# Joining weight bits with two one-input 16-bit passes, and normalising both attention heads on GpSimd

## The chip, the cores and the metric

The kernel runs on one core of a Trainium2 chip. The metric is the device time of one execution in microseconds; lower is better. The core has TensorE (PE, with PEld for its weight loads), VectorE (DVE), ScalarE (ACT), GpSimd (POOL) and the queues that issue transfers (here SyncE, SP). Each engine works through its own instructions in program order and waits for others on semaphores.

## The reference, cut to what matters

```python
def attention(q, k, v):                     # batch 2, 12 heads, 448 positions, head size 64
    scores = causal_mask(q @ k.T / 8)       # masked entries: -1e9
    scores = scores - scores.max(-1)
    attn = exp(scores)
    attn = attn / (attn.sum(-1) + 1e-9)     # the normalising
    return attn @ v                         # 896 tokens x 768

def moe(x):                                 # w_in 768x2048, w_out 2048x768
    h = x @ w_in
    return (h * clip(h + 3, 0, 6) / 6) @ w_out

def moe2(x):                                # w_gate, w_val 768x1536, w_out 1536x768
    xn = x / sqrt(mean(x*x) + 1e-6) * rms_g
    return (silu(xn @ w_gate) * (xn @ w_val)) @ w_out

out = moe2(moe(attention(q, k, v)))
```

The weights arrive as 64-bit floats, q, k and v as 32-bit floats.

## The kernel before, in words

**Attention.** The work is cut into 24 units, each one batch, one pair of heads (j = 0 and 1) and one half g of the 448 query positions. Units 0 to 11 have g = 0 and rows of 112 and 224 keys (blocks i = 0 and 1), units 12 to 23 have g = 1 and rows of 336 and 448 keys. A unit goes through `a_scores` (S below: TensorE, L232), `a_mask` (DVE, L242, adds the mask and takes the row's extreme), `a_exp` (ACT, L249, which also sums the row), `a_sums` (DVE, L257 and L258: the reciprocals of the sums), `a_norm` (L268: each row times its reciprocal; head 0 on DVE, head 1 on GpSimd, two instructions a head), `a_transpose` (T below: TensorE, L284, one call a head), `a_evict` (ACT, L294, copies the transposed rows out of PSUM), `a_values` (V below: TensorE, L310), `a_x` (ACT, L320) and `a_xlow` (DVE, L326).

**Weights.** Each piece of the weights is a tile `raw` of 128 x 768 64-bit floats, seen as 768 pairs of 32-bit words, low and high. `w_split` makes a 32-bit float of each: ACT scales the high words into `c` (L134), DVE shifts the low words right by 29 (L135) and joins the sign bit of the high words to them (L136, two inputs), and a step later `w_join` shifts `c` left by 3 and joins these bits (L141). ACT then rounds `c` into `whi` (L150), and DVE takes `wlo` = c - whi (L156). 68 pieces are made in this way; 32 more are pieces kept in DRAM that come back as 32-bit floats and go straight to L150.

**Products.** Each product of the two networks is three matmuls (L174, L176, L178) on the high and low parts. Networks run after one another for the two halves g; the first product for g = 0 starts when the units with g = 0 are through, beside the attention of g = 1.

**Order.** The program order is written out by hand in steps. `at(delay, fn)` puts a call into a later step; within a step come first the calls that are due, then what `plan` holds for the step. Unit u starts at step 5u, with S there. T and V come at fixed steps after it, and `a_sums` at a fixed number of steps after `a_exp`, by a table over five phases (phase 0: units 0 to 8; phases 4, 3, 2: units 9, 10, 11; phase 1: units 12 to 20):

```python
SUMS = (4, 1, 1, 2, 3)
TRANSPOSES = (12, 8, 6, 9, 11)
VALUES = (19, 13, 9, 13, 17)
...
        at(0, a_norm, u, 0)
        at(1, a_norm, u, 1)
```

So T(0) stands on TensorE's queue between S(2) and S(3), and in general T(u) ahead of S(u+3) for the early units. From unit 9 on the distance between the normalising and T is shorter. No product stands on TensorE's queue before S(13); from there on 4.8 matmuls of the products are issued in each step beside the attention.

Of the kernel before, what the change touches and what calls it, by code (L numbers as in the profile page):

```python
# [9 lines left out]
F32 = mybir.dt.float32  # L10
F32R = mybir.dt.float32r
U32 = mybir.dt.uint32
AF = mybir.ActivationFunctionType
ALU = mybir.AluOpType

# [27 lines left out]
def fused_kernel(ctx: ExitStack, tc, qa, qb, ka, kb, v, w_in, w_out, w_gate, w_val, w_out2, rms_g, out):  # L43
# [5 lines left out]
    nc = tc.nc  # L49
# [10 lines left out]
    def slot(shape, name, dtype=F32):  # L60
        return pool.tile(shape, dtype, tag="a", name=name)

    def f32(ap):
        return ap.bitcast(F32)
# [15 lines left out]
    def at(delay, fn, *args):  # L80
        due[clock["now"] + delay].append((fn, args))
# [24 lines left out]
    def w_load():  # L106
# [4 lines left out]
        if srcs[n] is None:  # L111
# [3 lines left out]
            return  # L115
        t = wpool.tile([128, 768, 2], U32, tag="raw", name=f"raw{n}", bufs=NRAW)
        nc.sync.dma_start(t.rearrange("p n t -> p (n t)"), srcs[n].bitcast(U32))
        raws[n] = t

    def w_split():  # L120

        n = state["split"]
        if n >= len(srcs):
            return
        state["split"] += 1
        if n in plain:
            at(1, w_halves, n, plain.pop(n))
            return
        raw = raws.pop(n)
        low, high = raw[:, :, 0], raw[:, :, 1]  # L130
        c = wpool.tile([128, 768], F32, tag="c", name=f"c{n}", bufs=NC_BUF)


        nc.scalar.mul(c, f32(high), 2.0 ** -112)  # L134
        nc.vector.tensor_scalar(low, low, 29, None, op0=ALU.logical_shift_right)  # L135
        nc.vector.scalar_tensor_tensor(low, high, 0x80000000, low, ALU.bitwise_and, ALU.bitwise_or)  # L136
        at(1, w_join, n, c, low)

    def w_join(n, c, z):
        bits = c.bitcast(U32)  # L140
        nc.vector.scalar_tensor_tensor(bits, bits, 3, z, ALU.logical_shift_left, ALU.bitwise_or)  # L141
        if n < 4 * NP1:
            kept[n + NP1] = dram.tile([128, 768], F32, name=f"kept{n}")
            nc.sync.dma_start(kept[n + NP1], c)
        at(1, w_halves, n, c)
# [16 lines left out]
    def w_tile(n, j):  # L162

        if n not in used:
            used.add(n)
            splits.pop(n - 2, None)
            at(1, w_split)
        return tuple(t[:, j * 128:(j + 1) * 128] for t in splits[n])
# [78 lines left out]
    def a_exp(u, outs, last):  # L247
        for c, src, dst, n in outs:
            nc.scalar.activation(  # L249
                dst, dst, AF.Exp, scale=-1.0, bias=st[u][:, 0, c:c + 1],  # L250
                accum_out=st[u][:, 1, c:c + 1])
# [3 lines left out]
    def a_sums(u):  # L255
        t = st[u]
        nc.vector.tensor_scalar_add(t[:, 2], t[:, 1], 1e-9)  # L257
        nc.vector.reciprocal(t[:, 2], t[:, 2])  # L258
        at(0, a_norm, u, 0)
        at(1, a_norm, u, 1)  # L260

    def a_norm(u, j):
        g, b, p = units[u]
        for i in range(2):
            n = (2 * g + i + 1) * C
            t, o = sm[u, j][i]
            c = st[u][:, 2, 2 * j + i:2 * j + i + 1]
            (nc.vector, nc.gpsimd)[j].tensor_scalar_mul(t[:, o:o + n], t[:, o:o + n], c)  # L268

    def a_transpose(u, j):  # L270
        g, b, p = units[u]
# [69 lines left out]
    def ff1_relu(g, m, ps):  # L341
        t = slot([128, NT], f"t{g}_{m}")
        nc.scalar.activation(t, ps, AF.Relu, bias=half, scale=1.0 / 6.0)
        at(1, ff1_mul, g, m, ps, t)
# [27 lines left out]
    def ff1_y(g, m, ps):  # L372
        hi = slot([128, NT], f"yhi{g}_{m}", F32R)
        nc.scalar.mul(hi, ps, gvec[:, m:m + 1])
        s = slot([128, NT], f"sq{g}_{m}")
        nc.scalar.activation(s, ps, AF.Square)
        at(1, ff1_ylow, g, m, ps, hi, s)
# [17 lines left out]
    def rms_root(g, ps):  # L395
        nc.scalar.activation(ri[g], ps, AF.Sqrt, bias=eps, scale=1.0 / DM)
        at(1, rms_inv, g)
# [26 lines left out]
    def ff2_silu(t):  # L424
        nc.scalar.activation(t, t, AF.Silu)

# [36 lines left out]
    with tc.manual_schedule():  # L463
# [41 lines left out]
        for n in range(NW - 1):  # L505
            plan[30 + 16 * n].append((0, w_split))
# [73 lines left out]
```

## Time and profile before

| | us |
|---|---|
| median of 3 runs | 614.26 (614.22 to 614.49) |
| profiled execution, whole time | 613.24 |
| profiled execution, span from first to last instruction | 611.5 |
| mean granted TensorE clock | 0.992 |
| TensorE busy | 599.3 (98%) |
| DVE busy | 430.4 (70%) |
| ACT busy | 303.4 (50%) |
| POOL busy | 122.3 (20%) |

The shares are means over stages that differ: attention alone (to about 53 us), attention beside the first product (to about 166 us), and products alone (to the end).

### The profile page before, as it was taken

To read this page: it belongs to the slowest core of one execution; us is meant where nothing else is said; L and a number is where in the kernel's file an instruction comes from. 1 tells how busy PE (TensorE), PEld (TensorE's weight loads), DVE (VectorE), ACT (ScalarE), POOL (GpSimd) and SP (SyncE) were. 2 spreads that over 40 slices of the span, in tenths; PEclk is the share of its full clock that TensorE was granted. 3 is DMA by queue.
4 is the path that set the end of the run, shared out by engine and by line. 5 is a ranking of instruction groups with operands and counts; after the bars stand their busy time and mean duration, and the time that the engine had idled before them with its cause. 6 is when DMAs were issued, how large, how long until landed. Compare 5 with 4: busy or idle time off the path is not lost.

```text
span 611.5 us, 8863 instructions
## 1 busy us (share of the span) xinstructions
PE 599.3 (98%) x3210; PEld 521.1 (85%) x3210; DVE 430.4 (70%) x763; ACT 303.4 (50%) x599; POOL 122.3 (20%) x108
## 2 busy tenths in 40 slices
PE   8879999999999999999999999999999999999997
PEld 6545767676899999999999999999999999999996
DVE  4879999998444499995444977777777777555520
ACT  5978878787644565554333653343334344222200
POOL 3434333241123331011010111111111112100000
PEclk9889999999999999999999999999999999999999
DMA  8468758564133648985435523332333333244100
GB/s 226 135 205 239 252 182 275 179 219 133 59 98 108 229 154 284 330 295 179 126 86 206 194 96 117 103 105 103 104 104 107 114 116 124 96 144 144 53 32 30
DMA packets 31931, 92.98 MB, mean 152 GB/s; under 512 B 4624, under 2 KB 13648, under 8 KB 31888
## 3 DMA queue, kind: packets, MB, share of 16 engines
q1 hardware_dynamic: 31888, 92.42, 46.3%
q8 instruction: 25, 0.41, 0.3%
q14 instruction: 18, 0.15, 0.1%
HBM read 77.07 MB, written 15.34 MB: 151 GB/s over the span
## 4 chain that ended last, share of the span: by engine, by line
PE 93%; ACT 4%; DVE 1%; DMA 0%; issue 0%; POOL 0%; DVEq 0%; ACTq 0%; POOLq 0%
PE f L174 10%; PE f L178 9%; PE f L176 9%; PE h L176 7%; PE h L178 7%; PE h L174 6%; PE y L174 6%; PE y L178 6%; PE y L176 6%; PE o L174 5%; PE o L178 5%; PE o L176 5%; PE s L232 4%; PE o L310 4%; PE t L284 3%; ACT sm L249 3%
## 5 line engine op out<-in xcount | busy, mean ns | idle before, releaser
L150 ACT CAST whi<-c 128x768 fp32r<-128x768 f32 x100 | 83.5, 835 | 125.7 <-DVE c L141 106.8
L156 DVE TENSOR_TENSOR wlo<-c,whi 128x768 fp32r<-128x768 f32 x100 | 97.1, 971 | 23.6 <-ACT whi L150 21.6
L174 PE MATMUL f<-yhi,whi 128*128 128x448 f32 x288 | 105.8, 367 | 0.0
L178 PE MATMUL f<-yhi,wlo 128*128 128x448 f32 x288 | 104.9, 364 | 0.0
L176 PE MATMUL f<-ylo,whi 128*128 128x448 f32 x288 | 104.0, 361 | 0.0
L268 POOL TENSOR_SCALAR sm<-sm,st 112x112 f32<-112x112 f32 (+3 forms) x48 | 54.9, 1154 | 100.3 <-DVE st L258 29.1
L136 DVE SCALAR_TENSOR_TENSOR raw<-raw 128x768 uint32<-128x768 uint32 x68 | 73.1, 1075 | 2.3
L176 PE MATMUL h<-xl,whi 128*128 128x448 f32 x192 | 72.1, 375 | 0.0
L174 PE MATMUL h<-xh,whi 128*128 128x448 f32 x192 | 71.3, 371 | 0.0
L178 PE MATMUL h<-xh,wlo 128*128 128x448 f32 x192 | 71.0, 370 | 0.0
L174 PE MATMUL y<-ghi,whi 128*128 128x448 f32 x192 | 70.5, 367 | 0.0
L178 PE MATMUL y<-ghi,wlo 128*128 128x448 f32 x192 | 70.0, 365 | 0.0
L176 PE MATMUL y<-glo,whi 128*128 128x448 f32 x192 | 69.3, 361 | 0.0
L141 DVE SCALAR_TENSOR_TENSOR c<-c,raw 128x768 uint32<-128x768 uint32 x68 | 65.8, 968 | 2.7 <-ACT c L134 0.4
L134 ACT ACTIVATE c<-raw 128x768 f32<-128x768 f32 x68 | 61.9, 910 | 1.3 <-DMA raw<-in_w_out 1.3
L358 POOL TENSOR_TENSOR slo<-u,shi 128x448 fp32r<-128x448 f32 x24 | 31.2, 1300 | 145.8 <-ACT shi L436 145.8
L178 PEld LDWEIGHTS f<-yhi,wlo 128*128 128x128 f32 x288 | 53.9, 187 | 5.4 <-issue 0.2
L176 PEld LDWEIGHTS f<-ylo,whi 128*128 128x128 f32 x288 | 54.1, 188 | 4.0
L174 PEld LDWEIGHTS f<-yhi,whi 128*128 128x128 f32 x288 | 54.1, 188 | 3.7 <-issue 0.2
L249 ACT ACTIVATE sm<-sm,st 112x112 f32<-112x112 f32 (+3 forms) x96 | 49.7, 519 | 14.6 <-DVE st L242 14.5
L174 PE MATMUL o<-shi,whi 128*128 128x448 f32 x144 | 52.9, 367 | 0.0
L178 PE MATMUL o<-shi,wlo 128*128 128x448 f32 x144 | 52.3, 363 | 0.0
(61 smaller groups left out, 929.3 us busy)
## 6 DMA issues: line engine op xcount, KB each, us to landing
raw<-in_w_out SPq DMA_DIRECT2D x28, 768.0 KB, 5.0
raw<-in_w_in SPq DMA_DIRECT2D x16, 768.0 KB, 5.1
kept<-c SPq DMA_DIRECT2D x32, 384.0 KB, 2.7
c<-kept SPq DMA_DIRECT2D x32, 384.0 KB, 3.1
raw<-in_w_gate SPq DMA_DIRECT2D x12, 768.0 KB, 4.4
raw<-in_w_val SPq DMA_DIRECT2D x12, 768.0 KB, 4.3
k<-in_kb SPq DMA_DIRECT2D x24, 112.0 KB, 4.3
v<-in_v SPq DMA_DIRECT2D x12, 224.0 KB, 3.8
```

The source lines that it names most:

```text
L134: nc.scalar.mul(c, f32(high), 2.0 ** -112)
L136: nc.vector.scalar_tensor_tensor(low, high, 0x80000000, low, ALU.bitwise_and, ALU.bitwise_or)
L141: nc.vector.scalar_tensor_tensor(bits, bits, 3, z, ALU.logical_shift_left, ALU.bitwise_or)
L150: nc.scalar.copy(hi, c)
L156: nc.vector.tensor_sub(lo, c, f32(hi))
L174: nc.tensor.matmul(ps, whi, xhi, start=first, stop=False)
L176: nc.tensor.matmul(ps, whi, xlo, start=False, stop=False)
L178: nc.tensor.matmul(ps, wlo, xhi, start=False, stop=last)
L232: nc.tensor.matmul(ps[:C, o:o + n], tq[64 * j:64 * j + 64, i * C:(i + 1) * C], tk[64 * j:64 * j + 64, 0:n], start=True, stop=True)
L249: nc.scalar.activation(dst, dst, AF.Exp, scale=-1.0, bias=st[u][:, 0, c:c + 1], accum_out=st[u][:, 1, c:c + 1])
L268: (nc.vector, nc.gpsimd)[j].tensor_scalar_mul(t[:, o:o + n], t[:, o:o + n], c)
L358: (engine or nc.gpsimd).tensor_sub(lo, t, f32(hi))
```

## The change

The two DVE passes that prepare the low words become two passes over 16-bit words with one input each. Word 1 of the four 16-bit words of a 64-bit float, shifted right by 13, goes to word 0; the top bit of word 3 goes to word 1. The 32-bit low word then holds the same bits as before. And `a_norm` runs on GpSimd for both heads, as one instruction with two multiplications: by the row's reciprocal, then by 1.0.

```diff
+U16 = mybir.dt.uint16
...
         nc.scalar.mul(c, f32(high), 2.0 ** -112)
-        nc.vector.tensor_scalar(low, low, 29, None, op0=ALU.logical_shift_right)
-        nc.vector.scalar_tensor_tensor(low, high, 0x80000000, low, ALU.bitwise_and, ALU.bitwise_or)
+
+        words = raw.rearrange("p n t -> p (n t)").bitcast(U16).rearrange("p (n w) -> p n w", w=4)
+        nc.vector.tensor_scalar(words[:, :, 0], words[:, :, 1], 13, None, op0=ALU.logical_shift_right)
+        nc.vector.tensor_scalar(words[:, :, 1], words[:, :, 3], 0x8000, None, op0=ALU.bitwise_and)
         at(1, w_join, n, c, low)
...
-            (nc.vector, nc.gpsimd)[j].tensor_scalar_mul(t[:, o:o + n], t[:, o:o + n], c)
+            nc.gpsimd.tensor_scalar(t[:, o:o + n], t[:, o:o + n], c, 1.0, op0=ALU.mult, op1=ALU.mult)
```

## Rows read from the trace of the kernel before

**Rows 1.** The page: busy times by engine, and the chain that ended last.
```profile
PE 599.3 (98%) x3210; PEld 521.1 (85%) x3210; DVE 430.4 (70%) x763; ACT 303.4 (50%) x599; POOL 122.3 (20%) x108
...
PE 93%; ACT 4%; DVE 1%; DMA 0%; issue 0%; POOL 0%; DVEq 0%; ACTq 0%; POOLq 0%
```

**Rows 2.** Busy time by stretch: engines in us, granted clock, DMA share, GB/s.
```profile
0.00:50.00 50.00, 42.30 (x304) 29.16 (x304) 35.99 (x171) 38.25 (x141) 19.05 (x34) 0.90 0.68 198
50.00:100.00 50.00, 49.12 (x299) 34.85 (x299) 49.30 (x112) 40.60 (x96) 19.70 (x12) 1.00 0.71 228
```

**Rows 3.** The same columns, by single microseconds.
```profile
25.00:26.00 1.00, 1.00 (x6) 0.81 (x6) 1.00 (x3) 1.00 (x6) 0.00 (x0) 0.59 0.92 257
...
32.00:33.00 1.00, 1.00 (x13) 0.58 (x10) 0.26 (x2) 1.00 (x4) 0.54 (x1) 0.99 0.94 346
```

**Rows 4.** Timeline of TensorE: start, duration, instructions, idle time before and releaser.
```profile
24.89 1.35 PE L284 MATMUL t<-ident,sm 112*112 112x112 f32 x6 [1.76 <-DVE sm L268]
...
38.42 1.69 PE L310 MATMUL o<-pt,v 112*64 112x224 f32 x8 [2.54 <-ACT pt L294]
...
50.88 0.78 PE L310 MATMUL o<-pt,v 112*64 112x224 f32 x6 [1.10 <-ACT pt L294]
```

**Rows 5.** Lines 135 and 136: duration in ns, min/median/max.
```profile
L135 DVE TENSOR_SCALAR raw<-raw x68: 532/555/1532, 20.6 to 579.3; 128x768 uint32<-128x768 uint32 x68
...
L136 DVE SCALAR_TENSOR_TENSOR raw<-raw x68: 958/961/1801, 21.2 to 579.9; 128x768 uint32<-128x768 uint32 x68
```

**Rows 6.** The chain that ended last, 34 to 37 us: start, us, what.
```profile
34.20 0.43 DVE sm L268 x2
34.64 0.48 DVE raw L135
...
35.14 0.97 DVE raw L136
...
36.21 0.97 DVE c L141
```

**Rows 7.** Timeline of DVE: a normalising that stands ahead of the next mask.
```profile
42.43 0.62 DVE L268 TENSOR_SCALAR sm<-sm,st 112x112 f32<-112x112 f32 x2
```

**Rows 8.** Groups of POOL by form, 5 to 22 us: busy us, mean ns.
```profile
L268 POOL TENSOR_SCALAR sm<-sm,st 112x224 f32<-112x224 f32 x5 | 4.2, 844 | 0.0
L268 POOL TENSOR_SCALAR sm<-sm,st 112x112 f32<-112x112 f32 x5 | 2.8, 566 | 11.2 <-DVE st L242 10.0 <-DVE st L258 1.2
```

**Rows 9.** Groups of POOL by form, 74 to 160 us.
```profile
L268 POOL TENSOR_SCALAR sm<-sm,st 112x448 f32<-112x448 f32 x9 | 14.7, 1634 | 0.0
L268 POOL TENSOR_SCALAR sm<-sm,st 112x336 f32<-112x336 f32 x9 | 12.3, 1364 | 58.7 <-ACT pt L294 16.5 <-PE o L310 14.8 <-DVE st L258 9.3
```

**Rows 10.** POOL over the whole span: two memsets, by form.
```profile
L474 POOL MEMSET mask<- 112x448 f32 x1 | 0.5, 472 | 0.0
...
masks.py:197 POOL MEMSET ident<- 128x128 f32 x1 | 0.2, 205 | 0.3 <-POOLq L569 0.3
```

**Rows 11.** Line 386: an addition of two tensors on POOL, ns min/median/max.
```profile
L386 POOL TENSOR_TENSOR sq<-sq,sq x10: 1153/1165/1442, 250.4 to 346.3; 128x448 f32<-128x448 f32 x10
```

**Rows 12.** Timeline of the first units, 9 to 14 us.
```profile
9.11 1.39 POOL L268 TENSOR_SCALAR sm<-sm,st 112x112 f32<-112x112 f32 x2 [6.97 <-DVE st L242]
...
9.83 0.80 DVE L268 TENSOR_SCALAR sm<-sm,st 112x112 f32<-112x112 f32 x2
...
11.24 0.24 DVE L242 CUSTOM_DVE_ANT_0 sm<-s,mask 112x112 f32<-112x112 f32 x1
...
11.30 0.83 PE L232 MATMUL s<-k,q 64*112 64x112 f32 x8
...
13.64 0.24 DVE L242 CUSTOM_DVE_ANT_0 sm<-s,mask 112x112 f32<-112x112 f32 x1
```

**Rows 13.** Timeline of unit 12: head 1's normalising on POOL, head 1's T.
```profile
51.95 2.97 POOL L268 TENSOR_SCALAR sm<-sm,st 112x336 f32<-112x336 f32 x2 [4.86 <-DVE st L258]
...
55.75 0.45 PE L284 MATMUL t<-ident,sm 112*112 112x112 f32 x3
```

## The prediction

> **What bounds the kernel now.** I read the page first. TensorE is busy for 98% of the span and makes up 93% of the chain that ended last [rows 1], so a faster DVE or a busier GpSimd counts only where TensorE waits. The table by stretch says where that is: in the first 50 us TensorE is busy for 42.3 us at a granted clock of 0.90; from 50 to 100 us it is busy for 49.1 us at 1.00, although DVE is busy for 49.3 us there [rows 2]. So the change is decided in the first 53 us or so, while attention for g = 0 runs alone. Behind that, what DVE is spared is hidden under TensorE, and only a new wait could cost.
>
> Inside the first stretch I read the timeline and the chain. From 9 to 20 us the first masks of two successive units start 2.40 us apart (11.24 and 13.64) [rows 12]. The loop is on DVE and ACT: `a_sums` waits for the exponentials, stands ahead of the next mask, and that mask releases the next exponentials. The normalising stands behind the mask on DVE, so it isn't in this loop. From 20 us on the weight pieces come in between. TensorE idles 1.76 us before 24.89, 2.54 us before 38.42 and 1.10 us before 50.88 [rows 4]. Behind the first of these idle times the granted clock falls (0.59 in the microsecond from 25) and is back at 0.99 in the one from 32 [rows 3]. A V took 1.69 us from 38.42, against 0.83 us for an S at full clock [rows 4, 12].
>
> **The 16-bit passes.** L135 goes, at 0.555 us in the median, and L136, at 0.961 us [rows 5]: 1.52 us for each of 68 pieces. Two one-input passes come. No row shows a 16-bit pass on this engine. The nearest is L135 itself: the same operation on the same 768 elements, one input, the same step of 8 bytes in and out. 768 elements in 0.532 us at best is more than one a nanosecond, against 0.958 for the two-input pass, so I take 0.56 us for each new pass, 1.11 for both: 0.40 us less a piece. Bounds: not above L136's 0.96 each, which makes it 0.40 more a piece; below, half of L135 (0.28 each), if 2-byte elements went twice as fast, which makes it 0.96 less. I keep L135's, since the step is unchanged. L141, L134 and the semaphores stay as they are, and no transfer is moved.
>
> The Trainium skill, VectorE: DVE Perf Modes (What auto-detection actually checks), says that the double rate for 16-bit data needs a step of 1, while a single-source pass from SBUF to SBUF can double its rate whatever its element size. By that the new passes would cost what L135 costs, the value taken; no row here shows a 16-bit pass to test it.
>
> Where it counts: in the chain from 34.20, the normalising of head 0 (0.43), L135 (0.48), L136 (0.97) and L141 (0.97) follow one another and end in the V at 38.42 [rows 4, 6]. L136 becomes a pass of 0.56: **-0.40 us**. The piece split at 21 us gains nothing: there L141 waits for ACT's `c`. From 57 us on there are some 65 more pieces, 26 us less DVE work, all counted at nothing: TensorE's queue is full there and covers it [rows 2]. If that cover were gone, each piece would be worth 0.4 us.
>
> **Head 0's normalising leaves DVE.** In the chain it is 0.43 us at 34.20 [rows 6]: **-0.43**. For units 9 to 11 `a_sums` comes earlier in the table, and the normalising stands ahead of the next mask on DVE: 0.62 us at 42.43 [rows 7], 0.55 from start to start. Two such units lie on the loop. The exponentials there queue behind ACT's copies too, so I count half: **-0.5**. In the g = 1 units it is hidden.
>
> **Both heads on GpSimd.** The price of the new form decides. The one-multiplication form takes 0.566 us for 112 columns and 0.844 for 224 [rows 8]: 2.48 ns a column above 0.29 us, so 1.41 for the pair of one head. Extended to 448 columns that is 1.40 us, and beside DVE's passes the mean was 1.63 [rows 9]. Against this stand two rows of the same engine. An addition reads two tensors of 448 columns and takes 1.165 us [rows 11]: less, for twice the input. And memsets rise by 0.83 ns a column (472 against 205 ns, 320 columns apart) [rows 10]. So reading and writing aren't what holds the one-multiplication form to 2.48 ns; its loop is. The new form may run in that loop (same price), pay a second time for the second multiplication, or run in another loop nearer to the port. Bounds: 0.83 ns a column above 0.29 (0.38 and 0.47, a pair 0.85, both heads 1.7 us), and twice 2.48 ns (0.84 and 1.40, a pair 2.24, both heads 4.5). At the old price both heads take 2.8.
>
> I take the lower end, 1.7 us for both heads, on the ground of rows 10 and 11; it is the most uncertain choice here, and both ends stay in the range. Then the norms of unit 0 are through at 9.11 + 1.7 = 10.8 us instead of 10.63 for DVE's [rows 12]. S(3) behind that T ends at 12.13, and the mask that needs it starts at 13.64, so 1.5 us of room covers it. 1.7 is below the loop's 2.40, so no lag grows. GpSimd has nothing else queued until 166 us, so no other wait stands behind it.
>
> The Trainium skill, GPSIMD Engine Reference (3.1 Elementwise; 4.1 Engine selection), says that one-input work runs at roughly line rate and bodies of up to two operations at 1.03 cycles a column. At its 1.2 GHz that is 0.86 ns, an estimate. The trace disagrees for the one-multiplication form (2.48 ns). By the rule the sum is the one below; by the row it is the rival's.
>
> **The clock.** T(5) at 24.89 waits for DVE's normalising, which stands behind a join and four masks, with 1.76 us of idle time [rows 4]. On GpSimd it no longer stands behind them, and T(5) could start some 0.9 us earlier. An idle time of 0.9 us is under the 1.10 us before 50.88; the clock was 1.00 over the 50 us that follow that one [rows 2, 4]. If the fall at 25 us goes, one V and one S at half clock on the chain go back to full: 1.69 / 2 + 0.83 = 1.7 us. I count half: **-0.8**.
>
> **Sum.** -0.40 - 0.43 - 0.5 - 0.8 = -2.1 us against the profiled execution's 613.24, so 611.1. The median lies 1.0 above that execution, so 612.0 as a median.
>
> **Rivals.**
> *A: GpSimd becomes the bound (slower).* If two multiplications cost what one does, both heads take 2.82 us a unit against a loop of 2.40. It decides from 1.20 us a pair upward. Each of the five units before the first split falls back another 0.42: the last norms of unit 4 are through at 9.11 + 5 x 2.82 = 23.2 us. Late next are T, the copies behind it on ACT, and L134 behind these. Of the 2.9 us I count 2.5. Units 9 to 11, whose T follows closely, add about 1. In unit 12 head 1 is through at 51.95 + 2 x 2.82 = 57.6, where its T started at 55.75 [rows 13]: 1.8. Less the gains of DVE (1.3): +4.0, so 617.2 profiled, 618.2 as a median. For it: the nearest row is the old form. Against: that form is slower than an addition of two tensors. The same Trainium skill page (8. Key points) has DVE as about twice as fast for elementwise work, which speaks for A; for the old form the trace agrees: 1.39 us for a pair on GpSimd against 0.80 on DVE [rows 12].
> *C: each multiplication pays.* Both heads at 4.5 us a unit: 12 units end at 9.11 + 54 = 63 us instead of 47, so +15, about 629. The g = 1 units, at 8.9 us, would still fit.
> *D: nothing measurable.* The new passes cost 0.96 each, so -0.43 + 0.40 in the chain and only the -0.5 remains; or ACT, busy for 38 of the first 50 us [rows 2], ends last anyway and the gains on DVE are hidden. Then 613.3 to 614.2.
>
> **How the numbers follow.** The forecast (lower end on GpSimd) has 0.50, D 0.15, A 0.25, C 0.10. A measurement of this kernel can tell about 0.2%, 1.2 us, from no change. So faster 0.50, same 0.16 (D and the edge of the forecast), slower 0.34 (A and C). The forecast's own range is 609.2 to 613.3: from 16-bit passes at half price with the whole clock gain (-0.56 and -0.9 more, and as much again in the loop) to no clock gain and half of the rest. For 8 in 10 the range reaches through D and A and leaves out C: 609.2 to 619.0.
>
> **What would show it.** L136's line as a TENSOR_SCALAR of about 0.55 us; L268 on POOL alone, 96 times, with 112 columns near 0.38 and 224 near 0.47 (A: 0.57 and 0.84; C: 0.84 and 1.40); first masks still 2.40 apart; the idle time before the V of 38.42 shorter by about 0.8; a clock of 1.00 in the microseconds from 25 to 32; V and S there at 0.8 to 1.0 us. Behind 57 us TensorE's rows should repeat, only earlier. The prediction is wrong if a T waits for POOL in the first 20 us, or if T of unit 12 does.

## The result, and the profile after

The changed kernel takes 618.14 us in the median of 4 runs (617.62 to 618.47), the kernel before 614.38 beside it: a ratio of 1.006, with a 95% interval of 1.0043 to 1.0078. It is slower by 3.8 us, where 2.1 us less was forecast. The profiled execution took 618.13 us, with a span of 616.3 against 611.5. All line numbers from L135 on stand one to three higher than before: L138 and L139 are the two 16-bit passes, L144 is `w_join`, L159 `wlo`, L271 the normalising, L245 the mask, L287 is T and L313 is V.

The page after, the parts that answer to [rows 1]: busy times, and the chain that ended last by engine.

```profile
PE 601.7 (98%) x3210; PEld 520.8 (84%) x3210; DVE 446.9 (73%) x715; ACT 302.5 (49%) x599; POOL 137.7 (22%) x156
...
PE 79%; DVE 12%; ACT 5%; issue 1%; DMA 1%; POOL 0%; DVEq 0%; SPq 0%; ACTq 0%; POOLq 0%
```

DVE runs 48 instructions fewer (head 0's normalising) and is busy for 16.5 us more. Its share of the chain that ended last went from 1% to 12%. Lines 138 and 139 after, which answer to [rows 5] (ns, min/median/max):

```profile
L138 DVE TENSOR_SCALAR raw<-raw x68: 993/1045/2016, 21.0 to 584.2; 128x768 uint16<-128x768 uint16 x68
...
L139 DVE TENSOR_SCALAR raw<-raw x68: 1023/1049/1765, 22.1 to 585.3; 128x768 uint16<-128x768 uint16 x68
```

A 16-bit pass takes 1.05 us, not the 0.56 that was taken, and more than the 0.96 that was set as the upper bound. A piece costs 2.09 us where it cost 1.52. GpSimd after, in groups by form over the whole span, and the first two of its rows in the timeline, which answer to [rows 8, 9] and [rows 12]:

```profile
L271 POOL TENSOR_SCALAR sm<-sm,st 112x448 f32<-112x448 f32 x24 | 24.9, 1039 | 0.0
...
L271 POOL TENSOR_SCALAR sm<-sm,st 112x336 f32<-112x336 f32 x24 | 21.9, 911 | 64.5 <-ACT pt L297 24.2 <-PE t L287 13.7 <-ACT sm L252 9.1
...
L271 POOL TENSOR_SCALAR sm<-sm,st 112x224 f32<-112x224 f32 x24 | 12.3, 514 | 0.0
L271 POOL TENSOR_SCALAR sm<-sm,st 112x112 f32<-112x112 f32 x24 | 8.6, 358 | 25.7 <-DVE st L261 15.1 <-DVE st L245 10.6
```

```profile
10.18 1.54 POOL L271 TENSOR_SCALAR sm<-sm,st 112x112 f32<-112x112 f32 x4 [8.04 <-DVE st L245]
12.57 1.54 POOL L271 TENSOR_SCALAR sm<-sm,st 112x112 f32<-112x112 f32 x4 [0.84 <-DVE st L245]
```

Both heads of an early unit take 1.54 us, against 1.39 for one head before. GpSimd idles 0.84 us between units, which follow one another by 2.39 us as before. So GpSimd isn't the bound.

Where the time went shows when the same matmul, counted in order, is looked up in both traces. At 9 us, just behind the first scores, a matmul comes 1.07 us later, because the first scores start later; from 70 us on the delay is 1.41; it stays there until 249 us, and between 250 and 276 us it grows to 4.8, where it stays to the end. The stretch from 230 to 280 us, of the kernel before and then of the changed one (busy us of PE, PEld, DVE, ACT, POOL with counts; clock; DMA):

```profile
230.00:280.00 50.00, 50.00 (x249) 46.35 (x248) 46.91 (x59) 28.03 (x39) 6.63 (x6) 1.00 0.84 292
```

```profile
230.00:280.00 50.00, 47.82 (x233) 42.57 (x231) 49.59 (x55) 25.32 (x35) 9.10 (x5) 1.00 0.81 280
```

This is the third product (`ff1_out` for g = 0, tiles y), which uses 16 pieces made by the two passes. TensorE gets 16 matmuls fewer done, at 0.2 us each 3.2 us of work. DVE was busy for 46.9 of 50 us there before, and is busy for 49.6 now. The waits after, from 240 to 300 us (total us, times, longest), and the chain there:

```profile
ACT whi L153 <- DVE c L144: 24.9, 12, 3.1
PEld y L181 <- DVE wlo L159: 4.5, 10, 1.1
...
PE y L181 <- DVE wlo L159: 2.3, 3, 0.8
```

```profile
244.76 0.97 DVE raw L138
...
245.76 1.06 DVE raw L139
...
246.86 0.73 DVE wlo L159
247.59 0.86 DVE c L144
248.45 0.98 DVE raw L138
```

One piece takes DVE 3.69 us from start to start (244.76 to 248.45). TensorE needs 18 matmuls for a piece: at 249 in 50 us, 3.61 us. On top DVE takes 0.6 us for `ylo` after every 48 matmuls. For these 48, with 2.67 pieces, TensorE needs 9.6 us and DVE 2.67 x 3.69 + 0.6 = 10.4; with 0.58 us less a piece, as before, it was 8.9. So the old passes fitted and the new ones don't. From 230 to 290 us DVE's idle time falls from 7.9 to 2.0 us.

Last, TensorE's idle times, as in [rows 4], after:

```profile
25.61 0.78 PE L287 MATMUL t<-ident,sm 112*112 112x112 f32 x6 [1.36 <-DVE st L245]
27.69 1.72 PE L313 MATMUL o<-pt,v 112*64 112x224 f32 x8 [1.29 <-ACT pt L297]
...
40.20 1.18 PE L313 MATMUL o<-pt,v 112*64 112x224 f32 x8 [2.66 <-ACT pt L297]
```

T(5) waits 0.4 us less than before, now for a mask (L245) and no longer for the normalising, but the V behind it then waits 1.29 us for ACT's copy, where it waited 0.28, and the clock falls again (that V took 1.72 us).

### The profile page after: what moved, and what is told of

Its sections match the earlier page's. It is cut to its first block, busy times and chain, and to the rows that moved or that the text cites. A ratio compares the mean times of both kernels' runs of the same rounds, so it can differ in the third digit from the quotient of the medians.

```text
span 616.3 us, 8909 instructions
## 1 busy us (share of the span) xinstructions
PE 601.7 (98%) x3210; PEld 520.8 (84%) x3210; DVE 446.9 (73%) x715; ACT 302.5 (49%) x599; POOL 137.7 (22%) x156
## 4 chain that ended last, share of the span: by engine, by line
PE 79%; DVE 12%; ACT 5%; issue 1%; DMA 1%; POOL 0%; DVEq 0%; SPq 0%; ACTq 0%; POOLq 0%
PE f L177 10%; PE f L181 9%; PE f L179 9%; PE h L179 5%; PE h L181 5%; PE h L177 5%; PE o L177 5%; PE o L181 5%; PE o L179 5%; PE y L181 4%; PE y L177 4%; PE y L179 4%; PE s L235 3%; PE o L313 3%; ACT sm L252 3%; DVE raw L138 3%
## 5 line engine op out<-in xcount | busy, mean ns | idle before, releaser
L159 DVE TENSOR_TENSOR wlo<-c,whi 128x768 fp32r<-128x768 f32 x100 | 97.7, 979 | 26.0 <-ACT whi L153 24.1
L271 POOL TENSOR_SCALAR sm<-sm,st 112x112 f32<-112x112 f32 (+1 forms) x96 | 66.1, 705 | 90.2 <-ACT pt L297 24.2
L139 DVE TENSOR_SCALAR raw<-raw 128x768 uint16<-128x768 uint16 x68 | 78.9, 1160 | 2.3
L138 DVE TENSOR_SCALAR raw<-raw 128x768 uint16<-128x768 uint16 x68 | 79.0, 1161 | 0.0
L144 DVE SCALAR_TENSOR_TENSOR c<-c,raw 128x768 uint32<-128x768 uint32 x68 | 66.6, 980 | 3.6 <-ACT c L135 1.1
L135 ACT ACTIVATE c<-raw 128x768 f32<-128x768 f32 x68 | 61.7, 908 | 0.0
```

Source lines behind the costliest of these rows:

```text
L138: nc.vector.tensor_scalar(words[:, :, 0], words[:, :, 1], 13, None, op0=ALU.logical_shift_right)
L139: nc.vector.tensor_scalar(words[:, :, 1], words[:, :, 3], 0x8000, None, op0=ALU.bitwise_and)
L159: nc.vector.tensor_sub(lo, c, f32(hi))
L271: nc.gpsimd.tensor_scalar(t[:, o:o + n], t[:, o:o + n], c, 1.0, op0=ALU.mult, op1=ALU.mult)
```

## The experiments

Theory 1: the 16-bit passes cost the time, by making DVE the last in the third product. Theory 2: both heads on GpSimd cost it, the prediction's rival A; its 618.2 us is the time that was measured. Theory 3: the later start belongs to the change's code. In all, ratios are to the kernel before, run beside them on the same chip (medians of 613.4 and 613.75 us there; 613.45, one execution, beside the last experiment). A kernel that ran once has no ratio: it is there for what its instructions cost.

**Only the normalising.** The changed kernel with the old join:

```diff
-        nc.vector.tensor_scalar(words[:, :, 0], words[:, :, 1], 13, None, op0=ALU.logical_shift_right)
-        nc.vector.tensor_scalar(words[:, :, 1], words[:, :, 3], 0x8000, None, op0=ALU.bitwise_and)
+        nc.vector.tensor_scalar(low, low, 29, None, op0=ALU.logical_shift_right)
+        nc.vector.scalar_tensor_tensor(low, high, 0x80000000, low, ALU.bitwise_and, ALU.bitwise_or)
```

> Only the normalising on GpSimd as in the changed kernel; the old 32-bit join. Theory 1 (the 16-bit passes cost the time: at 1.05 us each they make DVE the last in the third product): no waits of TensorE for wlo between 240 and 280 us, both heads 1.54 us on GpSimd, 613.0 to 614.0 us, at or a little under the kernel before. Theory 2 (both heads on GpSimd cost the time, T waits for GpSimd): 616 us or more. Theory 3 (the 1.07 us by which the first scores start later belong to the change's code): first scores at about 6.0 us again in this kernel or in the next; by theory 1 that is a load that came later by chance, and the start is 5.4 us in at least one of them.

Measured: 611.98 us, ratio 0.9962 (0.9948 to 0.9977). The third product, in the same columns as above, is whole again:

```profile
230.00:280.00 50.00, 50.00 (x249) 46.35 (x248) 47.90 (x59) 27.42 (x38) 6.88 (x5) 1.00 0.83 290
```

So the normalising is a gain, by itself larger than the expected 613.0 to 614.0 us, and theory 2 falls. In this profile too the first mask started late, at 7.28 us (7.48 in the changed kernel, 6.41 before).

**Only the 16-bit passes.** The changed kernel with head 0's normalising back on DVE:

```diff
-            nc.gpsimd.tensor_scalar(t[:, o:o + n], t[:, o:o + n], c, 1.0, op0=ALU.mult, op1=ALU.mult)
+            (nc.vector, nc.gpsimd)[j].tensor_scalar_mul(t[:, o:o + n], t[:, o:o + n], c)
```

> Only the two 16-bit passes; head 0 back on DVE with one multiplication. Theory 1: the passes at 1.05 us each, TensorE idle some 3 us or more for wlo between 240 and 280 us, 618 to 619 us, as slow as the changed kernel or slower, since head 0 is on DVE as well. Theory 2: 614 to 615 us.

Measured: 620.32 us, ratio 1.0104 (1.009 to 1.0119), above the expected 618 to 619. The first mask started at 6.11 us, although this kernel has the new passes. In the profiles of the seven kernels that follow, the first mask starts between 6.20 and 7.04 us, in no order that goes with an edit; theory 3 falls. The waits from 240 to 300 us are those of the changed kernel:

```profile
PEld y L181 <- DVE wlo L159: 4.6, 9, 1.1
...
PE y L181 <- DVE wlo L159: 2.3, 3, 0.8
```

Matched in order against the kernel before, this profile is 3.3 us late from 72 us on and 7.0 us late at 276 us: 3.7 us of it in the third product, 3.3 in the attention, where DVE has to carry head 0's normalising as well and the clock was at its half level for 13.7 us behind 38 us.

**Both heads on GpSimd with one multiplication**, with the old join, which is rival A by itself:

```diff
-            (nc.vector, nc.gpsimd)[j].tensor_scalar_mul(t[:, o:o + n], t[:, o:o + n], c)
+            nc.gpsimd.tensor_scalar_mul(t[:, o:o + n], t[:, o:o + n], c)
```

> The old 32-bit join, both heads on GpSimd with the old one-multiplication form. If that form keeps its 0.57 and 0.84 us, both heads take 2.8 us a unit against a loop of 2.4, and the prediction's rival A says 617 us (its 618.2 as a median), T waiting for GpSimd in the first 30 us. If the second multiplication is not what makes the new form cheap, both heads take 1.5 us and the time is that of the kernel with the new form alone.

Measured: 615.67 us, ratio 1.0034 (1.0022 to 1.0046). POOL's groups by form from 5 to 22 us, its first row in the timeline, and the waits of TensorE up to 70 us:

```profile
L268 POOL TENSOR_SCALAR sm<-sm,st 112x224 f32<-112x224 f32 x9 | 7.6, 841 | 0.0
L268 POOL TENSOR_SCALAR sm<-sm,st 112x112 f32<-112x112 f32 x10 | 5.9, 592 | 7.4 <-DVE st L242 6.9 <-DVE st L258 0.5
```

```profile
8.99 10.89 POOL L268 TENSOR_SCALAR sm<-sm,st 112x112 f32<-112x112 f32 x16 [6.86 <-DVE st L242]
```

```profile
PEld t L284 <- POOL sm L268: 12.6, 22, 1.5
...
PE t L284 <- POOL sm L268: 4.1, 6, 1.0
```

GpSimd works through 16 instructions, four units, without a gap, and T waits for it. So rival A's mechanism exists and costs 2.3 us (A said 4.0); the second multiplication takes it away. Against the normalising alone, with two multiplications, the single multiplication costs 3.7 us. It isn't what slowed the changed kernel.

**Two one-input 32-bit passes.** The changed kernel, with passes of the price that the prediction took:

```diff
-        nc.vector.tensor_scalar(words[:, :, 0], words[:, :, 1], 13, None, op0=ALU.logical_shift_right)
-        nc.vector.tensor_scalar(words[:, :, 1], words[:, :, 3], 0x8000, None, op0=ALU.bitwise_and)
+        nc.vector.tensor_scalar(low, low, 29, None, op0=ALU.logical_shift_right)
+        nc.vector.tensor_scalar(low, low, 7, None, op0=ALU.bitwise_and)
```

> The changed kernel with both passes as 32-bit one-input passes; the second keeps the lower three bits and leaves the sign bit out, so the weights lose their signs. This gives the passes the price that the prediction took for them (0.56 us each). Theory 1: both passes 0.53 to 0.58 us, no waits for wlo, 611.5 to 613.5 us, under the kernel before. Theory 2: 616 us or more.

Measured: 610.0 us, ratio 0.9944 (0.9923 to 0.9965), a little under the expected stretch. The two passes, in groups of DVE by form (these are means; the medians are 0.555 and 0.563 us, and L135's mean before was 0.681):

```profile
L137 DVE TENSOR_SCALAR raw<-raw 128x768 uint32<-128x768 uint32 x68 | 46.9, 690 | 1.5 <-DMA raw<-in_w_out 1.5
L138 DVE TENSOR_SCALAR raw<-raw 128x768 uint32<-128x768 uint32 x68 | 46.4, 683 | 2.3
```

So with passes at the price that the prediction took, the kernel gains 3.4 us at the medians. Part of this is the clock: three of its six executions kept it at 1.00 (608.9 to 609.2 us), the other three took 610.8 to 612.2. Matched in order against the kernel before, this profile gains 2.5 us up to 100 us and nothing behind that.

**What makes a 16-bit pass slow.** First, a 32-bit pass that moves words and a 16-bit pass that doesn't:

```diff
...
+        nc.vector.tensor_scalar(low, high, 0x80000000, None, op0=ALU.bitwise_and)
+        nc.vector.tensor_scalar(words[:, :, 1], words[:, :, 1], 0x8000, None, op0=ALU.bitwise_and)
```

> The changed kernel with two other passes in place of the two: one of 32 bits that takes the high words' sign bits to the low words (input and output differ), then one of 16 bits in place on word 1. The bits of the low words are lost, so the weights are rounded to fewer bits. If moving between words is what costs, the 32-bit pass takes 1.0 us and the 16-bit pass in place 0.55. If 16-bit elements at this step are what costs, the 32-bit pass takes 0.55 us and the 16-bit pass in place 1.05.

```profile
L138 DVE TENSOR_SCALAR raw<-raw x68: 530/555/1525, 19.8 to 575.8; 128x768 uint32<-128x768 uint32 x68
...
L139 DVE TENSOR_SCALAR raw<-raw x68: 1025/1051/1920, 20.3 to 576.3; 128x768 uint16<-128x768 uint16 x68
```

Moving costs nothing; the 16-bit elements at this step do. (One execution: 609.65 us, at a granted clock of 1.00 throughout the 50 us of attention alone.) Then 16-bit passes over the same number of elements, but in neighbouring pairs:

```diff
...
+        nc.vector.tensor_scalar(words[:, 0:384, 0:2], words[:, 0:384, 0:2], 7, None, op0=ALU.bitwise_and)
+        nc.vector.tensor_scalar(words[:, 384:768, 0:2], words[:, 384:768, 0:2], 7, None, op0=ALU.bitwise_and)
```

> The changed kernel with two other 16-bit passes: each works in place on 384 pairs of neighbouring 16-bit words, 768 elements again (they keep three bits of each word; signs and other low bits are lost). If 2-byte elements alone are slow, 1.05 us each. If what counts is that elements of 2 bytes lie apart, they take 0.55 us or less.

```profile
L138 DVE TENSOR_SCALAR raw<-raw x68: 330/355/1322, 20.2 to 575.9; 128x768 uint16<-128x768 uint16 x68
...
L139 DVE TENSOR_SCALAR raw<-raw x68: 346/355/1320, 20.4 to 576.1; 128x768 uint16<-128x768 uint16 x68
```

0.355 us for 768 elements (one execution: 609.8 us). So 16-bit elements are fast in pairs and slow one by one, at four words apart. The Trainium skill, VectorE: DVE Perf Modes (What auto-detection actually checks), gives 16-bit single-source passes of step 1 the highest rate, which the 0.355 agrees with, and doubles single-source passes from SBUF to SBUF without asking for the element size, which the 1.05 at a step of four words doesn't bear out.

**The two-multiplication form for head 1 alone**, the kernel before otherwise:

```diff
...
+            if j == 0:
+                nc.vector.tensor_scalar_mul(t[:, o:o + n], t[:, o:o + n], c)
+            else:
+                nc.gpsimd.tensor_scalar(t[:, o:o + n], t[:, o:o + n], c, 1.0, op0=ALU.mult, op1=ALU.mult)
```

> The kernel before with the form of two multiplications for head 1 alone; head 0 stays on DVE. Theory: the gain of the normalising comes from DVE, which is freed of head 0, so this is the same as the kernel before, within 0.6 us. Rival: it comes from head 1's shorter time on GpSimd (0.87 instead of 1.41 us a unit), and the time is 1 to 2 us under the kernel before.

Measured: 613.76 us, ratio 0.9989 (0.9973 to 1.0006), no difference that can be told. The gain of the normalising comes from freeing DVE of head 0; the cheaper form is what lets GpSimd take it.

**The 16-bit passes everywhere but in the third product:**

```diff
...
+        if 2 * NP1 <= n < 3 * NP1:
+            nc.vector.tensor_scalar(low, low, 29, None, op0=ALU.logical_shift_right)
+            nc.vector.scalar_tensor_tensor(low, high, 0x80000000, low, ALU.bitwise_and, ALU.bitwise_or)
+        else:
...
```

> The changed kernel, but the 16 pieces of the third product (240 to 290 us) are joined by the old 32-bit passes; the other 52 by the 16-bit passes. Theory: the 3.3 us that TensorE loses there go, so 614 to 615 us, within 0.2% of the kernel before. Rival: the loss comes back in another product, 617 us or more.

Measured: 612.5 us, ratio 0.9984 (0.9967 to 1.0001). The stretch from 230 to 280 us:

```profile
230.00:280.00 50.00, 50.00 (x249) 46.34 (x249) 47.24 (x59) 27.86 (x38) 6.85 (x5) 1.00 0.82 287
```

The loss of the third product is gone and doesn't come back in another. The time is below the 614 to 615 us that were expected: six of the 12 executions had a mean clock of 0.996 or 0.999 and took 611.3 to 611.6 us, the other six 613.4 to 614.7. With 52 of the 68 pieces joined by slow passes the kernel is no slower than the one before, but it also has the gain of the normalising, which here makes up for what those passes cost in the attention (below).

**Other forms of two operations on GpSimd**, head 0 as multiply and add 0.0, head 1 as multiply by 1.0 and then by the reciprocal, with the old join:

```diff
...
+            if j == 0:
+                nc.gpsimd.tensor_scalar(t[:, o:o + n], t[:, o:o + n], c, 0.0, op0=ALU.mult, op1=ALU.add)
+            else:
+                nc.gpsimd.tensor_scalar(t[:, o:o + n], t[:, o:o + n], 1.0, c, op0=ALU.mult, op1=ALU.mult)
```

> The old 32-bit join, both heads on GpSimd; head 0 as a multiplication by the reciprocal and an addition of 0.0, head 1 as a multiplication by 1.0 and then by the reciprocal. If any two real operations take the cheap loop, all rows of 112 columns take 0.36 us and all of 224 take 0.50, as with two multiplications; if only that one form does, one of the heads takes 0.57 and 0.84 or more.

POOL's groups by form, 5 to 22 us (L269 is head 0, L271 head 1):

```profile
L271 POOL TENSOR_SCALAR sm<-sm,st 112x224 f32<-112x224 f32 x5 | 2.6, 527 | 0.0
L269 POOL TENSOR_SCALAR sm<-sm,st 112x224 f32<-112x224 f32 x5 | 2.2, 447 | 0.0
L271 POOL TENSOR_SCALAR sm<-sm,st 112x112 f32<-112x112 f32 x5 | 1.8, 358 | 0.0
L269 POOL TENSOR_SCALAR sm<-sm,st 112x112 f32<-112x112 f32 x5 | 1.8, 354 | 10.9 <-DVE st L242 9.9 <-DVE st L258 1.0
```

All three forms of two operations that were run are cheaper than the one multiplication; multiply and add is the cheapest by a little (one execution: 611.8 us).

## Why the prediction was wrong

**The 16-bit pass.** The step that failed: "I take 0.56 us for each new pass", with "not above L136's 0.96 each" as the bound. It measured 1.05. The nearest row had the same step in bytes, but elements of four bytes, and the bound was taken from another instruction without a reason why a pass with one input could not be slower. With that price the sign of the term turned: 0.58 us more a piece in place of 0.40 less.

**The cover.** The step that turned the dearer pass into a loss: "TensorE's queue is full there and covers it [rows 2]", for all pieces behind 57 us. At the price taken the cover does hold: with two 32-bit passes nothing changes behind 100 us. At the price measured it doesn't. The rows named for it end at 100 us, and full for TensorE doesn't say how near DVE is to its own end. In the third product DVE had 3.1 of 50 us left. The text priced the loss of the cover at 0.4 us a piece, and rival D took passes of 0.96 us, but D asked only about the chain at 34 us. (By the account of 48 matmuls above, passes of 0.96 us would need 2.67 x 3.52 + 0.6 = 10.0 us of DVE against TensorE's 9.6, an estimate: D too would have lost time there.) At 0.58 us more a piece the 16 pieces of the third product need 9.3 us more of DVE; 5.9 us of it fell into DVE's idle time, and 3.4 us came out on TensorE (3.7 with the passes alone). This is shown: the waits for `wlo` are there in both kernels with these passes in that product, and in none of those without.

In the attention the slow passes cost another 1.7 us: matched in order, from 70 us on the changed kernel is 1.9 us behind the one with the normalising alone, 0.2 of it from the later start; the two profiles start late alike (7.48 and 7.28 us) and spend 10.2 us each at half clock, though not in the same places. Two profiles that stay at full clock agree: the kernel with the old passes in the third product, which has both slow passes in the attention, falls 1.8 us behind the one with the moved 32-bit pass, which has one slow pass and one of 0.555 us. In both pairs 0.9 of it comes between 65 and 70 us, beside the first product, where the sum counted on the cover as well. There an S of the changed kernel waits for ACT's copies, and the chain behind these runs back over exponentials and `whi` to `c` (L144) on DVE:

```profile
69.68 0.81 PE L235 MATMUL s<-k,q 64*112 64x336 f32 x2 [0.23 <-ACT pt L297]
```

**GpSimd's price** was right: 0.36 and 0.51 us against 0.38 and 0.47, 1.54 against 1.7 for both heads, although the text called it its most uncertain choice and the split is another: 1.2 ns a column above 0.22 us, not 0.83 above 0.29. Why the form of one operation is the slower one is not shown. No lag grew. T's weight loads (PEld) waited for GpSimd, and its matmuls (PE) hardly did; from 0 to 62 us (total us, times, longest):

```profile
PEld t L287 <- POOL sm L271: 6.3, 13, 1.7
...
PE t L287 <- POOL sm L271: 0.4, 2, 0.2
```

Before, the weight loads of T waited 4.3 us for head 0 on DVE and 1.0 for head 1 on GpSimd, and the matmuls 3.3 us for DVE. The prediction named a T that waits for POOL in the first 20 us as a sign of being wrong: there the weight loads did wait, seven times, 2.2 us in all, but no matmul did. The rule of the Trainium skill, GPSIMD Engine Reference (3.1 Elementwise), 0.86 ns a column as an estimate, is nearer to the form of two operations ((493 - 358) / 112 = 1.2 ns, means from 5 to 22 us with the normalising alone) than to that of one (2.48).

**Head 0 off DVE** was right in direction: with the clock's term the forecast had 1.7 us for it, and the kernel with it alone gained 1.4 at the medians. Half of this is the clock: among executions at a mean of 0.991 to 0.992 the medians are 613.3 and 612.7 us, a gain of 0.7. The rest is that 5 of its 12 executions were at 0.997 or above, and none of the 17 of the kernel before beside it.

**The clock's term** was wrong in its mechanism. T(5) did start 0.4 us earlier, counted from the first scores, where 0.9 was taken; what it waits for by the trace is now a mask. The V behind it waits for ACT's copies, and these stand behind the exponentials; the idle time only moved behind T. Whether the clock falls there differs between executions of one and the same kernel, below; that it did so less often with the normalising alone makes the size of the term (0.8, against the 0.7 above) about right, by a way that was not found.

**Rival A** gave 618.2 us, and 618.14 was measured: the right time for a wrong reason. Without the experiment on the old form it would have passed for the cause. The range for 8 in 10, 609.2 to 619.0, reaches to the measured time only through A, so that it holds it is luck.

The kernel with the normalising alone beats both kernels: 611.98 us, 0.38% under the one before.

## What to carry to other kernels

When an edit changes the cost of an instruction that recurs over the whole span, price it against the stretch in which its engine is nearest to full, not the stretch in which the bound engine idles. An engine that nothing on the critical path waits for may still have only 6% of its time left. And a measured time that meets a rival's number is no evidence for that rival until its rows are looked at.

## What was not expected of the hardware

On DVE a pass over 768 single 16-bit elements, four words apart, takes 1.05 us, over 768 single 32-bit elements at the same step in bytes 0.555, and over 384 neighbouring pairs of 16-bit elements 0.355. On GpSimd a tensor times a per-row scalar takes 0.84 us for 224 columns as one operation and 0.45 to 0.53 us as two.

The granted clock differed between executions of the same kernel. With the normalising alone, the seven executions at a mean of 0.991 to 0.992 took 611.7 to 612.8 us, and the five at 0.997 to 1.000 took 609.5 to 610.0. On the chip of the later experiments three of 23 executions of the kernel before were at 0.994 or above (611.6 to 611.9 us). In the profiles with a lower mean the clock is at half its level in stretches between 14 and 52 us, behind idle times of TensorE. In the profile of the kernel that keeps the old passes in the third product, it stayed at full level throughout, behind idle times of 1.38 and 1.29 us. What decides it was not found.
